# The mixer's steps in the paired heads: from between the parts of the scores to behind the softmax and behind the taking

## The chip, the cores and the metric

One core of one Trainium2 chip runs the whole program. The metric is the device time of one execution in microseconds (us); the time before is the median of three runs.

## The reference

A decode step for 8 batches: attention over a cache of 8192 keys and values for 32 query heads that share 8 key/value heads, beside an MLP-mixer over the one token, both added to the input. Everything is float32.

```python
B, Sq, D = 8, 1, 512;  Hq, Hkv, Sk, Dh = 32, 8, 8192, 128;  F = 1792

def _A_ref(x, k_cache, v_cache, wq, wo):
    q = (x @ wq).reshape(B, Sq, Hq, Dh).transpose(0, 2, 1, 3)
    k = jnp.repeat(k_cache, rep, axis=1)
    v = jnp.repeat(v_cache, rep, axis=1)
    scores = jnp.einsum("bhqd,bhkd->bhqk", q, k) * (Dh ** -0.5)
    p = _softmax(scores, axis=-1)
    o = jnp.einsum("bhqk,bhkd->bhqd", p, v)
    return o.transpose(0, 2, 1, 3).reshape(B, Sq, Hq * Dh) @ wo

def _B_ref(x, w1, b1, w2, b2):
    h = _layernorm(x, axis=-1)
    u = jnp.einsum("bsd,sf->bdf", h, w1) + b1
    u = _gelu(u)
    y = jnp.einsum("bdf,fs->bds", u, w2) + b2
    return y.transpose(0, 2, 1)

x = A_x
xn = _layernorm(x, axis=-1)
return x + _A_ref(xn, ...) + _B_ref(xn, ...)
```

The caches are 8 x 8 x 8192 x 128 numbers each, 4 MB for the keys of one batch and one head, and as much for the values.

## The kernel before

**Stages.** First the queries of all heads are made. Then come the paired heads: heads 0 to 5 are worked two at a time, which gives 24 steps `duo_step(i)`, i = 0 to 23, with pair `g = i // 8` and batch `b = i % 8`. Heads 6 and 7 follow one by one in `pair(i)`, and the last two batches are written out by hand at the end. The order of every engine's instructions is the order in which the code issues them.

**The ring.** Keys and values live in a ring of five slots of 4 MB (`raw`). One load of a paired step is the keys, or the values, of two heads: 8 MB, two slots. Where the two slots wrap around the end of the ring, the load is split into two of 4 MB. `load_next` puts the next load on SP's queue; it can start when the last reader of its slots is done. In a step it is called once between the two halves of the keys (this loads the next step's keys) and once behind the first half of the products with the values (the next step's values). In steps 2, 9, 10, 17 and 18 a smaller load of output weights (`load_wo`, 1 MB) goes out on the same queue.

**A paired step.** The keys come in two halves, k = 0 and 1, and each half in two quarters. For each quarter DVE turns two pieces in place (`turn_duo`, L480, two transposes of 128x2048), then PE multiplies them with the queries (`qk_duo`, L491, 8 matmuls). Behind the four quarters stands `softmax_duo`: DVE's maximum (L500), a matmul that spreads it (L502), DVE's bias (L504), the exponential on ACT (L508), two matmuls that rearrange the result (L511) and two transposes into `pt` (L512). Then PE multiplies with the values in two halves (`pv_duo`, L523), between which every fourth step places the results of the four steps before (`place_duo`), and some steps project them (`o_project`, whose addition to `yrow` on DVE is L469). `take_duo` copies the result on ACT (L531).

**The mixer.** For each batch and each of the 14 slices of F, `mx_step` runs a gelu on ACT (L574) and a multiplication and an addition on POOL (L575, L576) into `macc`. There are 8 x 14 = 112 such steps; `mix(n)` runs the next n of them wherever it is called. Where a batch is through, `mix` first issues `mx_end`: a matmul on PE that reads `macc` (L580) and an addition to `yrow` on DVE (L581). Then `mx_begin` spreads the next batch's row by a matmul (L566) into the one buffer `hb` that the gelus read, and clears `macc` on POOL (L568). The paired steps call four mixer steps each, 96 in all, so an `mx_end` falls in paired steps 3, 7, 10, 14, 17 and 21. The remaining 16 run in the single heads.

ACT holds one set of function tables at a time: a table load stands ahead of the first gelu behind an exponential and ahead of the exponential behind a gelu.

Of the kernel before, what the change touches and what calls it, by code (L numbers as in the profile page):

```python
# [44 lines left out]
def attn_mixer_kernel(ctx: ExitStack, tc: tile.TileContext, x, kc, vc, wq, wo, w1, b1, w2, b2, out):  # L45
# [22 lines left out]
    def misc():  # L68
        return ps_m.tile([P, 512], F32, name="misc")

    def big():
        return t2k.tile([P, 512], F32, name="t2k")
# [42 lines left out]
    def load_next():  # L115
        if duo:
            load_duo()
        elif order:
            _, src, to, i = order.pop()
            h, b = divmod(i, B)  # L120
            t = slot().rearrange("p s (t d) -> p (s t) d", d=DH)
            rows = src[b, h].rearrange("(p t) d -> p t d", p=P)
            last = not order
            at = 0
            for n in PIECES if last else (NT,):
                nc.sync.dma_start(t[:, at:at + n, :], rows[:, at:at + n, :])
                at += n
            to[i] = t
            if last:
                load_wo(HKV - 1)  # L130
# [3 lines left out]
    def load_wo(h):  # L134
        t = place.tile([P, REP, D], F32, name="wo")
        if h < PAIRED:
            rows = wo[h // 2 * 2 * REP * DH:(h // 2 + 1) * 2 * REP * DH, :].rearrange("(p c) n -> p c n", p=P)
            rows = rows[:, h % 2 * REP:(h % 2 + 1) * REP, :]
        else:
            how = "(r p) n -> p r n" if h == HKV - 1 else "(p r) n -> p r n"  # L140
            rows = wo[h * REP * DH:(h + 1) * REP * DH, :].rearrange(how, p=P)
        for r in range(REP) if h == HKV - 1 else ():
            nc.sync.dma_start(t[:, r, :], rows[:, r, :])
        if h < HKV - 1:
            nc.sync.dma_start(t, rows)
        wos[h] = t
# [177 lines left out]
    def q_place_duo(g):  # L324
        m = misc()
        for q in range(NB):
            for s in range(2):
                nc.tensor.matmul(m[s * HP:(s + 1) * HP, q * B * REP:(q + 1) * B * REP], rep[:, q, :HP],
                                 QT[:, 2 * g + s].rearrange("p b r -> p (b r)"), start=True, stop=True)
        z_fill(m, 0)  # L330
# [134 lines left out]
    def o_project(h):  # L465
        m = misc()
        for r in range(REP):
            nc.tensor.matmul(m[:W, :], OT[h][:, r, :], wos[h][:, r, :], start=(r == 0), stop=(r == REP - 1))  # L468
        nc.vector.tensor_add(yrow, m[:W, :], yrow)  # L469
# [8 lines left out]
    def turn_duo(i, c):  # L478
        k = KP[i][c // NCH][:, c % NCH * CH_T:(c % NCH + 1) * CH_T, :].rearrange("p t d -> p (t d)")
        nc.vector.transpose(k, k)  # L480
# [3 lines left out]
    def qk_duo(i, k, cs):  # L484
        b = i % B
        if not k and not cs[0]:
            SD[i] = ps_a.tile([P, 512], F32, name="acc")
        t = KP[i][k]
        for q in range(NB):
            for c in cs:  # L490
                nc.tensor.matmul(SD[i][c * W:(c + 1) * W, :].rearrange("p (t j) -> p t j", j=W),  # L491
                                 Z[:, q, b, (1 - k) * REP:(1 - k) * REP + W],
                                 t[:, c * CH_T:(c + 1) * CH_T, q * W:(q + 1) * W],
                                 start=(not k and not q), stop=(k == 1 and q == NB - 1))

    def softmax_duo(i):
        b = i % B
        s = SD.pop(i)
        mr = work.tile([P, 1], F32, name="mr")
        nc.vector.tensor_reduce(mr, s, AX.X, ALU.max)  # L500
        m = misc()
        nc.tensor.matmul(m[:, :P], mr.to_broadcast([P, P]), ident, start=True, stop=True)  # L502
        nb = work.tile([P, 1], F32, name="nb")
        nc.vector.tensor_tensor_reduce(big()[:, :P], m[:, :P], hmask, -SCALE, 3.0e38, ALU.add, ALU.min, nb)  # L504
        p = big()
        if b % HB == 0:
            LD[i // HB] = work.tile([P, HB], F32, name="lr4")
        nc.scalar.activation(p, s, AF.Exp, bias=nb, scale=SCALE, accum_out=LD[i // HB][:, b % HB:b % HB + 1])  # L508
        for k in range(2):
            m = misc()  # L510
            nc.tensor.matmul(m, send[:, k, :], p, start=True, stop=True)  # L511
            nc.vector.transpose(PT[k][:, :CH_T * W], m)  # L512
# [3 lines left out]
    def pv_duo(i, k):  # L516
        b = i % B
        if not k:
            OD[i] = ps_a.tile([P, 512], F32, name="acc")
        v = VP[i][k].rearrange("p (c t) d -> p t c d", c=NCH)  # L520
        for t in range(CH_T):
            j = t % NB
            nc.tensor.matmul(OD[i][j * W:(j + 1) * W, :].rearrange("p (c d) -> p c d", c=NCH),  # L523
                             PT[k][:, t * W:(t + 1) * W], v[:, t],
                             start=(not k and t < NB), stop=(k == 1 and t >= CH_T - NB))

    def take_duo(i):
        g, b = divmod(i, B)
        if b % HB == 0:
            OBD[g] = one.tile([P, HB, 512], F32, name="ob")  # L530
        nc.scalar.copy(OBD[g][:, b % HB, :], OD.pop(i))  # L531
# [21 lines left out]
    def place_duo(i):  # L553
        g, b = divmod(i, B)
        if b == 0:
            OT[2 * g], OT[2 * g + 1] = OTS
        if b % HB == HB - 1:
            s, rl = place_all(OBD.pop(g), LD.pop(i // HB), 2 * REP)
            for x in range(2):
                put(OTS[x], b - HB + 1, s[:, :, x * REP:(x + 1) * REP], rl)  # L560
# [3 lines left out]
    def mx_begin(b):  # L564
        hb = ps_h.tile([P, D], F32, name="hb")
        nc.tensor.matmul(hb, ident[:B, b:b + 1].to_broadcast([B, P]), hn, start=True, stop=True)  # L566
        acc = one.tile([P, D], F32, name="macc")
        nc.gpsimd.memset(acc, 0.0)  # L568
        mx[b] = (hb, acc)

    def mx_step(b, j):
        hb, acc = mx[b]
        g = one.tile([P, D], F32, name="g")
        nc.scalar.activation(g, hb, AF.Gelu_apprx_tanh, bias=b1t[:, j:j + 1], scale=w1t[:, j:j + 1])  # L574
        nc.gpsimd.tensor_scalar(g, g, w2t[:, j:j + 1], 1.0, op0=ALU.mult, op1=ALU.mult)  # L575
        nc.gpsimd.tensor_add(acc, acc, g)  # L576

    def mx_end(b):
        m = misc()
        nc.tensor.matmul(m[:W, :], bsel[:, BO - BS * b:BO - BS * b + W], mx[b][1], start=True, stop=True)  # L580
        nc.vector.tensor_add(yrow, m[:W, :], yrow)  # L581
# [4 lines left out]
    def mix(n):  # L586
        for _ in range(n):
            b, j = divmod(step[0], NF)
            step[0] += 1
            if j == 0 and 0 < b <= B:  # L590
                mx_end(b - 1)
            if b < B:
                if j == 0:
                    mx_begin(b)
                mx_step(b, j)
# [4 lines left out]
    def duo_step(i):  # L600
        g, b = divmod(i, B)
        half = NCH // 2
        for k in range(2):
            for x in range(2):
                for c in range(half):
                    turn_duo(i, k * NCH + x * half + c)
                qk_duo(i, k, range(x * half, (x + 1) * half))
                mix(1)
            if not k:
                load_next()  # L610
                if i == N_PR - 1:
                    load_next()
        if i == N_PR - 1:
            load_next()
        del KP[i]
        softmax_duo(i)
        if b == B - 1 and g < PAIRED // 2 - 1:
            q_place_duo(g + 1)
        pv_duo(i, 0)
        load_next()  # L620
        if i:
            place_duo(i - 1)
        if g and b == 1:
            o_project(2 * g - 2)
            load_wo(2 * g - 1)
        if g and b == 2:
            o_project(2 * g - 1)
        if b == 2:
            load_wo(2 * g)
        pv_duo(i, 1)  # L630
        if i == N_PR - 1:
            load_next()
        del VP[i]
        take_duo(i)

    for i in range(N_PR):
        duo_step(i)
# [139 lines left out]
```

## Time and profile before

| what | value |
|---|---|
| median of 3 runs | 1306.81 us (1306.71 to 1308.07) |
| the profiled execution's own time | 1306.54 us |
| its span, first to last instruction | 1304.6 us |
| mean granted TensorE clock | 0.863 |
| busy PE, DVE, ACT, POOL | 945.8, 701.1, 229.0, 229.6 us |
| read from HBM | 553.69 MB, 424 GB/s over the span |

The page's first part gives busy time by engine, its fourth the chain of waits that ended last: one goes back from the last instruction to what released it, and so on to the start. A row of the chain has a start, a length and what took it; "DMA raw<-in_A_k_cache_dram" is the time from the issue of a load to its landing. Windows give for a stretch of the span the busy time of each engine (and instructions), the clock that was granted to PE, the share of the 16 DMA engines and what they moved. In the timeline a row ends with the idle time ahead of the instruction and what ended it.

### The profile page before, as it was taken

The numbers are of one execution on the slowest core, as the hardware profiler recorded it, in microseconds if no ns is written. First come the engines' busy times: TensorE is split into PE (matmuls) and PEld (weight loads), VectorE is DVE, ScalarE is ACT, GpSimd is POOL, SyncE is SP. The second block draws the span as 40 slices with busy tenths as digits, with TensorE's granted clock in tenths as the row PEclk, the third lists the DMA queues.
The fourth block names the chain that finished last, engine by engine and source line by source line (L and its number), as shares of the span: only waits on it lengthen the run. The fifth ranks groups of instructions, "written<-read, shape, count | busy, mean of one in ns | idle before, by whom it ended". The sixth has DMA issues, their size and how long they took to land.

```text
span 1304.6 us, 11227 instructions
## 1 busy us (share of the span) xinstructions
PE 945.8 (72%) x4782; PEld 259.4 (20%) x4782; DVE 701.1 (54%) x581; ACT 229.0 (18%) x321; POOL 229.6 (18%) x247
## 2 busy tenths in 40 slices
PE   2767866867786886886778787687777674665778
PEld 0211211211221221221122121121122121211223
DVE  3554625652745553565445655346565654566575
ACT  0212121110222122021211221102121332310000
POOL 1222112220222112122211222102221312100000
PEclk9878888988898898887889898788887877878889
DMA  9999999999999999998999999998999999999998
GB/s 400 438 445 424 441 429 436 433 431 439 387 449 420 443 426 437 423 441 374 417 448 422 431 425 429 426 440 362 421 444 418 434 434 433 432 434 434 431 431 344
DMA packets 15925, 554.41 MB, mean 425 GB/s; under 512 B 1884, under 2 KB 1916, under 8 KB 2692
## 3 DMA queue, kind: packets, MB, share of 16 engines
q1 hardware_dynamic: 15732, 553.67, 98.7%
q8 instruction: 37, 0.61, 0.2%
q14 instruction: 12, 0.10, 0.0%
q0 software_dynamic: 128, 0.02, 0.0%
q10 hardware_dynamic: 16, 0.02, 0.0%
HBM read 553.69 MB, written 0.02 MB: 424 GB/s over the span
## 4 chain that ended last, share of the span: by engine, by line
DMA 53%; PE 24%; DVE 21%; ACT 1%; issue 1%; POOL 0%; DVEq 0%; ACTq 0%; POOLq 0%
DMA raw<-in_A_k_cache_dram 49%; DVE raw L480 16%; PE acc L491 12%; PE acc L523 3%; DVE raw L336 3%; PE acc L414 3%; PE misc L511 2%; DMA raw<-in_A_v_cache_dram 2%; DMA b2t<-in_B_b_dram 2%; PE misc L540 1%; PE acc L347 1%; DMA wo<-in_A_wo_dram 1%; PE misc L297 1%; ACT L508 1%; PE misc L468 1%
## 5 line engine op out<-in xcount | busy, mean ns | idle before, releaser
L491 PE MATMUL acc<-raw,z 128*32 128x512 f32 x1536 | 405.0, 663 | 161.3 <-DVE raw L480 158.0
L480 DVE STREAM_TRANSPOSE raw<-raw 128x2048 f32<-128x2048 f32 x192 | 424.5, 2272 | 144.1 <-DMA raw<-in_A_k_cache_dram 144.1
L575 POOL TENSOR_SCALAR g<-g,pad 128x512 f32<-128x512 f32 x112 | 77.4, 691 | 742.5 <-ACT g L574 742.5
L491 PEld LDWEIGHTS acc<-raw,z 128*32 128x32 f32 x1536 | 95.0, 119 | 469.0 <-issue 292.4
L523 PE MATMUL acc<-raw,pt 128*32 128x512 f32 x1536 | 188.0, 631 | 0.0
L336 DVE STREAM_TRANSPOSE raw<-raw 128x2048 f32<-128x2048 f32 x64 | 145.6, 2293 | 60.2 <-DMA raw<-in_A_k_cache_dram 60.2
L576 POOL TENSOR_TENSOR macc<-macc,g 128x512 f32<-128x512 f32 x112 | 142.3, 1270 | 9.3
L574 ACT ACTIVATE g<-hb,pad 128x512 f32<-128x512 f32 x112 | 87.0, 777 | 214.1 <-POOL macc L576 165.5
L511 PE MATMUL misc<-t2k,send 128*128 128x512 f32 x96 | 76.7, 944 | 56.5 <-ACT t2k L508 56.5
L512 DVE STREAM_TRANSPOSE pt<-misc 128x512 f32<-128x512 f32 x48 | 34.4, 717 | 106.7 <-PE misc L511 106.2
L347 PE MATMUL acc<-raw,z 128*32 128x512 f32 x512 | 80.6, 626 | 10.3 <-DVE raw L336 8.1
L523 PEld LDWEIGHTS acc<-raw,pt 128*32 128x32 f32 x1536 | 47.8, 116 | 144.8 <-issue 114.1
L414 PE MATMUL acc<-raw,pt 128*32 128x512 f32 x480 | 76.5, 776 | 0.0
L508 ACT ACT_TABLE_LOAD x24 | 30.8, 1283 | 220.0 <-DVE nb L504 219.9
L500 DVE TENSOR_REDUCE mr<-acc 128x1 f32<-128x512 f32 x24 | 16.6, 691 | 92.5 <-PE acc L491 92.5
L364 PE MATMUL misc<-ident,mr 128*128 128x128 f32 x32 | 10.6, 424 | 74.9 <-DVE mr L359 74.9
L531 ACT COPY ob<-acc 128x512 f32<-128x512 f32 x24 | 14.0, 585 | 285.5 <-PE acc L523 285.5
L574 ACT ACT_TABLE_LOAD x32 | 41.1, 1283 | 32.6 <-PE hb L566 32.1
L511 PEld LDWEIGHTS misc<-t2k,send 128*128 128x128 f32 x96 | 23.0, 263 | 79.9 <-ACT t2k L508 61.1
L381 ACT ACTIVATE t2k<-acc,nb 128x512 f32<-128x512 f32 x16 | 11.0, 687 | 135.8 <-DVE nb L370 135.7
L568 POOL MEMSET macc<- 128x512 f32 x8 | 4.2, 524 | 156.1 <-PE misc L580 137.3
L347 PEld LDWEIGHTS acc<-raw,z 128*32 128x32 f32 x512 | 18.9, 113 | 60.9 <-issue 41.7
(117 smaller groups left out, 362.7 us busy)
## 6 DMA issues: line engine op xcount, KB each, us to landing
raw<-in_A_k_cache_dram SPq DMA_DIRECT2D x26, 4096.0 KB, 27.9
raw<-in_A_v_cache_dram SPq DMA_DIRECT2D x25, 4096.0 KB, 27.1
raw<-in_A_k_cache_dram SPq DMA_DIRECT2D x4, 2048.0 KB, 33.1
wo<-in_A_wo_dram SPq DMA_DIRECT2D x7, 1024.0 KB, 26.2
raw<-in_A_v_cache_dram SPq DMA_DIRECT2D x3, 1024.0 KB, 22.1
raw<-in_A_v_cache_dram SPq DMA_DIRECT2D x2, 512.0 KB, 25.6
wo<-in_A_wo_dram SPq DMA_DIRECT2D x4, 256.0 KB, 16.3
raw<-in_A_v_cache_dram SPq DMA_DIRECT2D x19, 25.6
```

The lines of the kernel that those rows point to most:

```text
L336: nc.vector.transpose(k, k)
L347: nc.tensor.matmul(S[i][c * W:(c + 1) * W, :].rearrange("p (t j) -> p t j", j=W), Z[:, q, b, REP:], k[:, c * CH_T:(c + 1) * CH_T, q * W:(q ...
L414: nc.tensor.matmul(O[i][j * W:(j + 1) * W, :].rearrange("p (c d) -> p c d", c=NCH), pt[:, t * W:(t + 1) * W], v[:, t], start=(t < NB), sto ...
L480: nc.vector.transpose(k, k)
L491: nc.tensor.matmul(SD[i][c * W:(c + 1) * W, :].rearrange("p (t j) -> p t j", j=W), Z[:, q, b, (1 - k) * REP:(1 - k) * REP + W], t[:, c * C ...
L508: nc.scalar.activation(p, s, AF.Exp, bias=nb, scale=SCALE, accum_out=LD[i // HB][:, b % HB:b % HB + 1])
L511: nc.tensor.matmul(m, send[:, k, :], p, start=True, stop=True)
L512: nc.vector.transpose(PT[k][:, :CH_T * W], m)
L523: nc.tensor.matmul(OD[i][j * W:(j + 1) * W, :].rearrange("p (c d) -> p c d", c=NCH), PT[k][:, t * W:(t + 1) * W], v[:, t], start=(not k an ...
L574: nc.scalar.activation(g, hb, AF.Gelu_apprx_tanh, bias=b1t[:, j:j + 1], scale=w1t[:, j:j + 1])
L575: nc.gpsimd.tensor_scalar(g, g, w2t[:, j:j + 1], 1.0, op0=ALU.mult, op1=ALU.mult)
L576: nc.gpsimd.tensor_add(acc, acc, g)
```

## The change

In `duo_step` the call `mix(1)` behind each quarter of the scores is taken out. A call `mix(2)` is put behind `softmax_duo` and another behind `take_duo`. The mixer steps per paired step stay four, and each `mx_end` stays in its step.

```diff
                 for c in range(half):
                     turn_duo(i, k * NCH + x * half + c)
                 qk_duo(i, k, range(x * half, (x + 1) * half))
-                mix(1)
             if not k:
                 load_next()
...
         del KP[i]
         softmax_duo(i)
+        mix(2)
         if b == B - 1 and g < PAIRED // 2 - 1:
             q_place_duo(g + 1)
         pv_duo(i, 0)
...
         del VP[i]
         take_duo(i)
+        mix(2)
```

DVE in paired step 14 before (L480 turns the keys `raw`, L581 is the addition of `mx_end` to `yrow`, L500 and L504 begin the softmax):

```order
L480 STREAM_TRANSPOSE raw<-raw 128x2048 x2
L581 TENSOR_TENSOR yrow<-misc,yrow 32x512
L480 STREAM_TRANSPOSE raw<-raw 128x2048 x6
L500 TENSOR_REDUCE mr<-acc 128x1
L504 ISA t2k,nb<-misc,hmask 128x128
```

and DVE in the same step now (L512 turns the probabilities into the two tiles `pt`):

```order
L480 STREAM_TRANSPOSE raw<-raw 128x2048 x8
L500 TENSOR_REDUCE mr<-acc 128x1
L504 ISA t2k,nb<-misc,hmask 128x128
L504 ISA nb 128x1
L512 STREAM_TRANSPOSE pt_156<-misc 128x512
L512 STREAM_TRANSPOSE pt_158<-misc 128x512
L581 TENSOR_TENSOR yrow<-misc,yrow 32x512
```

The addition moved from behind the first two turnings to behind the last transpose of the softmax; steps 7 and 21 read alike.

PE in step 14 before (L491 the scores, L580 the matmul of `mx_end`, L566 that of `mx_begin`, L502 and L511 those of the softmax):

```order
L491 MATMUL acc<-raw,z 32x512 x8
L580 MATMUL misc<-macc,bsel 32x512
L566 MATMUL hb<-hn,ident 128x512
L491 MATMUL acc<-raw,z 32x512 x24
L502 MATMUL misc<-ident,mr 128x128
```

and PE in the same step now (L523 the products with the values):

```order
L491 MATMUL acc<-raw,z 32x512 x32
L502 MATMUL misc<-ident,mr 128x128
L511 MATMUL misc<-t2k,send 128x512 x2
L580 MATMUL misc<-macc,bsel 32x512
L566 MATMUL hb<-hn,ident 128x512
L523 MATMUL acc<-raw,pt_156 32x512 x16
```

The two matmuls moved from between the scores to between the softmax and the products with the values.

DVE from the softmax of step 17 to the first turnings of step 18 now (L469 is the addition of `o_project`):

```order
L504 ISA nb 128x1
L512 STREAM_TRANSPOSE pt_156<-misc 128x512
L512 STREAM_TRANSPOSE pt_158<-misc 128x512
L469 TENSOR_TENSOR yrow<-misc,yrow 32x512
L581 TENSOR_TENSOR yrow<-misc,yrow 32x512
L480 STREAM_TRANSPOSE raw<-raw 128x2048 x8
```

where before step 17 had L581 within its own turnings, six of them ahead of it and two behind:

```order
L480 STREAM_TRANSPOSE raw<-raw 128x2048 x6
L581 TENSOR_TENSOR yrow<-misc,yrow 32x512
L480 STREAM_TRANSPOSE raw<-raw 128x2048 x2
L500 TENSOR_REDUCE mr<-acc 128x1
L504 ISA t2k,nb<-misc,hmask 128x128
```

The addition moved to behind the taking of step 17, ahead of the turnings of step 18; step 10 reads alike, and step 3 without an L469. The orders of POOL and SP did not change.

## The prediction

> **What bounds the kernel now.** I read the page first, then the chain of waits, then windows of 10 us, then the timeline around the places where the windows dip.
>
> ```profile
> q1 hardware_dynamic: 15732, 553.67, 98.7%
> DMA 53%; PE 24%; DVE 21%; ACT 1%; issue 1%; POOL 0%; DVEq 0%; ACTq 0%; POOLq 0%
> ```
>
> The loads on SP's queue fill 98.7% of the span, so only places where that queue runs empty can be won. In an undisturbed step the chain looks so (start, length, what):
>
> ```profile
> 278.22 4.52 DVE raw L480 x2
> 282.78 8.02 PE acc L491 x32
> 290.81 25.96 DMA raw<-in_A_k_cache_dram
> 316.87 4.51 DVE raw L480 x2
> ```
>
> The keys of paired step 6 are there at 278.22, those of step 7 at 316.87: 38.65 us for one load of keys and one of values, 19.3 each. The load of keys 7 is issued at 290.81, 12.6 after keys 6 came, when PE has read their first half (k=0). Steps 14 and 21 (the last three rows) look otherwise:
>
> ```profile
> 596.10 4.52 DVE raw L480 x2
> ...
> 605.39 0.68 DVE yrow L581
> ...
> 610.54 6.54 PE acc L491 x17
> 617.10 22.95 DMA raw<-in_A_k_cache_dram
> 640.13 4.52 DVE raw L480 x2
> ...
> 800.02 4.52 DVE raw L480 x2
> ...
> 840.99 17.67 DVE raw L480 x8
> ...
> 900.54 23.19 DMA raw<-in_A_k_cache_dram
> 923.83 4.52 DVE raw L480 x2
> ```
>
> Here `mx_end`'s addition to yrow (L581) stands between the turnings of keys: DVE waits from about 600.6 to 605.39 until PE is through the first quarter's scores and the product of `mx_end`, and the next load is issued 21.0 us after the keys came instead of 12.6. It then finds the queue empty: 22.95 and 23.19 us from issue to landing, where a load that follows another takes 19.3. So **a load costs nothing if it is issued 23.1 before it is due**: keys at 38.65 - 23.1 = 15.5 after the keys before (2.9 spare in step 6), values at 58.0 - 23.1 = 34.9 after the keys of the step that issues them. The windows (busy by engine, granted clock, DMA share, GB/s) show the holes:
>
> ```profile
> 340.00:350.00 10.00, 6.56 (x19) 2.16 (x16) 1.59 (x4) 2.06 (x3) 0.00 (x0) 0.84 1.01 433
> 350.00:360.00 10.00, 10.00 (x93) 3.25 (x94) 9.39 (x6) 2.65 (x6) 0.00 (x0) 0.99 0.96 383
> 610.00:620.00 10.00, 9.42 (x36) 2.58 (x38) 9.25 (x5) 2.33 (x3) 6.54 (x7) 0.68 0.57 216
> 750.00:760.00 10.00, 10.00 (x69) 2.80 (x62) 3.71 (x4) 0.11 (x1) 0.00 (x0) 1.00 0.98 390
> 890.00:900.00 10.00, 6.91 (x23) 1.71 (x25) 10.00 (x5) 3.61 (x4) 5.72 (x6) 0.66 0.59 256
> ```
>
> All four holes lie in or right behind a step with an `mx_end` (steps 7, 14, 17, 21). Steps 3 and 10 have one too, and spare time to swallow it.
>
> **The change, part by part.** The 96 mixer steps stay, four to a paired step, two behind the softmax and two behind the taking. Six `mx_end`s with the `mx_begin` behind them move: in steps 7, 14, 21 to behind the softmax, in 3, 10, 17 to behind the taking. In step 14 (the rows of DVE and PE stand with the change) all eight turnings of the keys now run without a wait for PE. L580 and L566 left the scores (L491) and stand ahead of the products with the values (L523), and the next load of values waits for those. Their price, and the marks I need, from the timeline:
>
> ```profile
> 299.59 0.69 DVE L500 TENSOR_REDUCE mr<-acc 128x1 f32<-128x512 f32 x1 [3.71 <-PE acc L491]
> 343.41 0.69 DVE L500 TENSOR_REDUCE mr<-acc 128x1 f32<-128x512 f32 x1 [3.71 <-PE acc L491]
> 354.91 0.33 SPq L105 DMA_DIRECT2D raw<-in_A_v_cache_dram  x1
> 717.52 13.28 DVE L480 STREAM_TRANSPOSE raw<-raw 128x2048 f32<-128x2048 f32 x6 [0.17 <-DMA raw<-in_A_k_cache_dram]
> 744.84 0.69 DVE L500 TENSOR_REDUCE mr<-acc 128x1 f32<-128x512 f32 x1 [5.19 <-PE acc L491]
> 753.02 0.33 SPq L105 DMA_DIRECT2D raw<-in_A_v_cache_dram  x1
> 880.73 4.50 DVE L480 STREAM_TRANSPOSE raw<-raw 128x2048 f32<-128x2048 f32 x2
> 887.89 0.59 PE L580 MATMUL misc<-macc,bsel 128*32 128x512 f32 x1
> 888.84 1.12 PE L566 MATMUL hb<-hn,ident 8*128 8x512 f32 x2
> 906.56 0.69 DVE L500 TENSOR_REDUCE mr<-acc 128x1 f32<-128x512 f32 x1 [3.71 <-PE acc L491]
> 916.37 0.33 SPq L105 DMA_DIRECT2D raw<-in_A_v_cache_dram  x1
> ```
>
> L580 and L566 take PE from 887.89 to 889.96, with one pass of scores among them (0.25, as 32 passes take 8.02 in step 6): 1.8 us, bounded above by twice that, 3.6, at half clock, and below by nothing, if PE only fills a wait with them. The softmax begins (L500) 299.59 - 278.22 = 21.4 after the keys in a step without a stall. Now step by step:
>
> - Step 7. Before, values 8 were issued at 354.91, landing 378.0, due 316.87 + 58.0 = 374.9: 3.1 lost. Now L500 comes at 338.3, 5.1 earlier, and the issue at 354.91 - 5.1 + 1.8 = 351.6 (353.4 at the upper price), landing at 374.7 (376.5): 0 lost (up to 1.6). Gain 3.1, at least 1.5.
> - Step 14. 640.13 - 596.10 - 38.65 = 5.4 lost. Now the keys are issued at 596.10 + 12.6 = 608.7, land by 631.8, due 634.8: gain 5.4.
> - Step 17. Values 18: 753.02 + 23.1 = 776.1, due 717.5 + 58.0 = 775.5, 0.6 lost. L500 comes 744.84 - 738.9 = 5.9 earlier: gain 0.6. By the keys it may be more: 800.02 - 717.52 = 82.5 for two steps, less 77.3, less 2.4 for the 1 MB of `wo` among them (an eighth of a load), is 2.8.
> - Step 21. 923.83 - 840.99 - 77.3 = 5.5 lost. Now keys 22 go out at 880.73 + 12.6 = 893.3, land by 916.4, due 840.99 + 77.3 = 918.3. Values 22 followed L500 by 9.8; now 902.1 + 9.8 + 1.8 = 913.7 (915.5), landing 936.8 (938.6), due 937.6: 0 lost (up to 1.0). Gain 5.5, at least 4.5.
> - Steps 3, 10: nothing was lost, nothing is gained.
>
> The sum is 3.1 + 5.4 + 0.6 + 5.5 = 14.6, at least 12.0, at most 16.8 with step 17's 2.8. Counted in undone bytes against 433 GB/s the four windows give (50 + 217 + 43 + 177) / 433 x 10 = 11.2. The first counts a late landing whole, part of which the queue may make good later; the second misses what lies outside the windows. I take 13.5, nearer to the landings, since the chain goes over these.
>
> What moves at no cost: the gelus on ACT between exponential and taking.
>
> ```profile
> 272.53 0.58 ACT L531 COPY ob<-acc 128x512 f32<-128x512 f32 x1 [9.13 <-PE acc L523]
> 273.13 1.28 ACT L574 ACT_TABLE_LOAD   x1
> ...
> 277.37 0.78 ACT L574 ACTIVATE g<-hb,pad 128x512 f32<-128x512 f32 x1 [2.17 <-POOL macc L576]
> ```
>
> A table load, two gelus and the wait for POOL are 5.0 us, inside the 9.13 that ACT idles before it takes; were they longer, the taking would be late, which frees one of four accumulators and holds no load. The tables still change twice a step. POOL's and SP's orders are unchanged. At step 7 the copies of the next heads' queries follow the gelus, ready before the products with the values end.
>
> Behind the taking (3, 10, 17) the addition waits for all products with the values, and the next keys' turnings are queued behind it on DVE. In step 17 L469, `o_project`'s addition, waited there already; L581 is what joined it.
>
> ```profile
> 200.93 4.50 DVE L480 STREAM_TRANSPOSE raw<-raw 128x2048 f32<-128x2048 f32 x2 [14.84 <-DMA raw<-in_A_k_cache_dram]
> 756.41 0.68 DVE L469 TENSOR_TENSOR yrow<-misc,yrow 32x512 f32<-32x512 f32 x1 [6.29 <-PE misc L468]
> 757.02 17.64 DVE L480 STREAM_TRANSPOSE raw<-raw 128x2048 f32<-128x2048 f32 x8
> 759.64 1.02 PE L491 MATMUL acc<-raw,z 128*32 128x512 f32 x2
> ```
>
> Behind step 17 PE ends about 759.6 - 5.9 = 753.7; with 1.8 and 0.7 the turnings begin near 756, not later than the 757.02 of before. Behind step 3 DVE idles 14.84 for the keys anyway. No cost.
>
> **The rivals.**
>
> *The clock eats half of it.* In step 14 the second quarter-scores took 6.54 in a window of clock 0.68, against 8.02 for two quarters in step 6: after a stall PE ran at half rate. If L580, L566 and the first products with the values all meet the half rate, the issue of values 8 and 22 is later by 1.8 + 2.5 (6.54 less half of 8.02): landing 379.0 and 941.1, 4.1 and 3.5 late, the sum 14.6 - 7.6 = 7.0, the time 1299.5. For it: PE idles through the exponential. Against it: the added products themselves fill PE there. The Trainium skill, "TensorE: Matmul & The Clock Gate", Part 1, says that an idle window of about 3.4 us halves the rate and a busy one restores it; the 0.68 beside 6.54 agrees. By that rule this rival needs an idle window ahead of L580; without one the sum stays. 12%.
>
> *The addition behind the taking holds the keys* (slower). If at 3, 10 and 17 DVE stood from the end of L512 to the end of PE's products, 6.3 (the wait of L469) + 3.2 (from its end of wait to 759.64) + 1.8 = 11.3, while the keys lay ready, each next load of keys would be 11.3 late, 2.9 of it spare: 8.4 x 3 = 25, less 14.6, so 1306.5 + 10.5 = 1317. It decides from keys that land over 4 us before PE is done. For it: L469's 6.29 shows this kind of hold. Against it: 14.84 in step 4, and the estimate of 756. The skill's same page (Part 1, "Architectural detail") has VectorE strictly first in, first out; the wait at 605.39 agrees. 6%.
>
> *Nothing comes of it.* The queue was 98.7% busy; what is not lost in the holes might be lost at other loads whose spare time the holes had refilled. Then 1306, within 2.6 us. Against it: the chain starts from a landing in each step, so all behind a hole shifts as one. 5%.
>
> **How the numbers follow.** The profiled execution took 1306.54, span 1304.6 and 1.9 outside, 0.3 under the median of 1306.81. 1306.5 - 13.5 = 1293.0, the likeliest case, 77%. Its own range is 1306.5 - 16.8 = 1290 to 1306.5 - 11.2 = 1295; with the clock's rival it reaches 1300, which leaves 11% out. Within 0.2%, 2.6 us, no change can be told. Faster 0.89, same 0.05, slower 0.06.
>
> **What would show it.** Right: no window of 10 us in the paired part under 400 GB/s; keys loads in steps 14 and 21 issued 12 to 13 after the keys; the wait of L581 for PE gone from the chain. The clock's rival: values 8 or 22 issued over 36 after their keys. The slower one: L480 behind L581 with no idle for keys, and new holes at steps 4, 11, 18. Wrong altogether: holes gone and the span unchanged.

## The result, and the profile after

The changed kernel takes 1294.13 us, the median of 4 runs (1293.01 to 1296.09), beside 1307.44 of the kernel before (4 runs, 1306.71 to 1308.79): a ratio of 0.9899, 95% interval 0.9882 to 0.9916. In a later comparison on one chip (experiment 10 below) it was 0.9905 (0.9885 to 0.9925). The forecast was 1293.0 in 1290 to 1300.

The profiled execution of after took 1296.09 us with a span of 1293.6, the longest of its four. From its page, the queue's row:

```profile
q1 hardware_dynamic: 15732, 553.67, 99.3%
```

The same 15,732 packets and 553.67 MB; the loads' share rose from 98.7% to 99.3%. The busy times of the engines changed little (PE 945.8 to 934.9 us, DVE 701.1 to 701.6): the kernel was bound by its loads and still is, with fewer holes. The chain around steps 14 and 21 (start, length, what):

```profile
595.68 4.51 DVE raw L480 x2
600.24 8.02 PE acc L491 x32
608.28 25.96 DMA raw<-in_A_k_cache_dram
634.33 4.52 DVE raw L480 x2
...
834.15 17.68 DVE raw L480 x8
...
873.62 4.41 DVE raw L480 x2
...
886.11 25.38 DMA raw<-in_A_k_cache_dram
911.58 4.52 DVE raw L480 x2
```

These now read like the undisturbed step 6: 32 passes of scores in one piece of 8.02, no L581 between, the next keys asked for 608.28 - 595.68 = 12.6 us after the keys came, and 634.33 - 595.68 = 38.65 us from keys to keys. Before, the distance was 44.03 there. At step 21, 911.58 - 834.15 = 77.4 for two steps, where 82.8 stood. The windows that had shown the holes, and one that still dips (busy by engine, granted clock, DMA share, GB/s):

```profile
350.00:360.00 10.00, 10.00 (x86) 3.01 (x78) 9.59 (x5) 3.73 (x8) 6.13 (x7) 1.00 1.07 455
430.00:440.00 10.00, 4.84 (x22) 0.80 (x16) 5.27 (x3) 2.05 (x3) 3.92 (x4) 0.74 0.90 390
610.00:620.00 10.00, 6.74 (x30) 1.64 (x26) 4.33 (x5) 1.29 (x2) 0.00 (x0) 1.00 1.00 433
890.00:900.00 10.00, 7.14 (x25) 1.94 (x22) 3.43 (x6) 0.78 (x2) 0.00 (x0) 1.00 1.00 433
```

The 216 and 256 GB/s of 610 to 620 and 890 to 900 are 433 now, the 383 at 350 is 455. The same work runs up to 12 us earlier in after, so a window does not hold quite the same piece of it; but between 270 and 960 us after has no window under 390. The timeline of after at two of the new places, step 7 (behind the softmax) and step 17 (behind the taking):

```profile
345.48 1.29 PE L580 MATMUL misc<-macc,bsel 128*32 128x512 f32 x2
346.70 1.12 PE L566 MATMUL hb<-hn,ident 8*128 8x512 f32 x2
346.81 0.68 DVE L581 TENSOR_TENSOR yrow<-misc,yrow 32x512 f32<-32x512 f32 x1 [0.50 <-PE misc L580]
352.04 0.33 SPq L105 DMA_DIRECT2D raw<-in_A_v_cache_dram  x1
...
749.99 0.68 DVE L581 TENSOR_TENSOR yrow<-misc,yrow 32x512 f32<-32x512 f32 x1 [3.61 <-PE misc L580]
750.60 17.64 DVE L480 STREAM_TRANSPOSE raw<-raw 128x2048 f32<-128x2048 f32 x8
```

Behind the softmax L581 waits 0.50 us for PE in step 7, where the first half of the next keys is already there (their turnings begin at 347.42, at once behind it). In steps 14 and 21 it waits 0.26, and the next keys come some 10 us later. Behind the taking of step 17 it still waits 3.61, and the turnings of the next keys, which lie ready, start at once behind it. In total VectorE (DVE in the rows) does not wait much less for this product. Groups of waits (total us, count, longest), before and then after:

```profile
DVE yrow L581 <- PE misc L580: 31.6, 8, 5.8
```

```profile
DVE yrow L581 <- PE misc L580: 23.8, 8, 8.1
```

7.8 us of waiting went, and 13 us of time: the gain must lie in which loads stand behind a wait more than in how long the engine waits. (In experiment 1 the sum is 6.9, and the time that of after.)

**Where the time came from.** One step's distance from keys to keys scatters by more than 1 us between executions, so I take stretches of the arrival of keys (the first turning, L480) that hold the moved work of one or two steps: keys 7, 11, 15, 19, 22. Those of before are 316.87, 477.53, 640.13, 800.02 and 923.83; of the profiled execution of after 316.90, 477.35, 634.33, 793.16 and 911.58. Keys 9 and 11 in the timeline of before and in the chain of after:

```profile
397.45 4.50 DVE L480 STREAM_TRANSPOSE raw<-raw 128x2048 f32<-128x2048 f32 x2 [7.64 <-DMA raw<-in_A_k_cache_dram]
...
477.53 17.64 DVE L480 STREAM_TRANSPOSE raw<-raw 128x2048 f32<-128x2048 f32 x8
```

```profile
395.91 4.52 DVE raw L480 x2
...
447.33 30.00 DMA raw<-in_A_k_cache_dram
477.35 4.52 DVE raw L480 x2
```

The chain of a second profiled execution of after (experiment 10, 1293.36 us, the lowest of its five runs, but nearer to the median):

```profile
316.75 17.68 DVE raw L480 x8
...
395.50 8.90 DVE raw L480 x4
...
446.80 28.37 DMA raw<-in_A_k_cache_dram
475.19 4.52 DVE raw L480 x2
...
593.60 8.90 DVE raw L480 x4
633.63 4.52 DVE raw L480 x2
...
791.01 4.52 DVE raw L480 x2
...
910.62 4.52 DVE raw L480 x2
```

| stretch | moved work in it | before | after | after again | gain (two executions) | forecast |
|---|---|---|---|---|---|---|
| keys 7 to 11 | steps 7, 10 | 160.66 | 160.45 | 158.44 | 0.2, 2.2 | 3.1 |
| keys 11 to 15 | step 14 | 162.60 | 156.98 | 158.44 | 5.6, 4.2 | 5.4 |
| keys 15 to 19 | step 17 | 159.89 | 158.83 | 157.38 | 1.1, 2.5 | 0.6 |
| keys 19 to 22 | step 21 | 123.81 | 118.42 | 119.61 | 5.4, 4.2 | 5.5 |
| sum | | 606.96 | 594.68 | 593.87 | 12.3, 13.1 | 14.6 |

The first row needs a second look. From keys 7 to keys 9, which hold step 7 alone, the three executions took 80.58, 79.01 and 78.75: 1.6 and 1.8 won, nearly the same twice. What sets the two executions of after apart comes later: the load of keys 11 went out 12.6 us after keys 10 (434.73 and 434.21) in both, and took 30.00 us in the one and 28.37 in the other. In before, keys 11 may have come a little before 477.53, since that row shows no wait for a load: the engine was at an addition of `o_project` until then.

### The profile page after: what moved, and what is told of

It reads as the page before. It is cut to its first block, busy times and chain, and to the rows that moved or that the text cites. A ratio compares the mean times of both kernels' runs of the same rounds, so it can differ in the third digit from the quotient of the medians.

```text
span 1293.6 us, 11227 instructions
## 1 busy us (share of the span) xinstructions
PE 934.9 (72%) x4782; PEld 258.5 (20%) x4782; DVE 701.6 (54%) x581; ACT 225.6 (17%) x320; POOL 230.1 (18%) x247
## 3 DMA queue, kind: packets, MB, share of 16 engines
q1 hardware_dynamic: 15732, 553.67, 99.3%
## 4 chain that ended last, share of the span: by engine, by line
DMA 52%; PE 24%; DVE 20%; ACT 1%; issue 1%; POOL 0%; DVEq 0%; ACTq 0%; POOLq 0%
DMA raw<-in_A_k_cache_dram 48%; DVE raw L480 15%; PE acc L491 11%; PE acc L523 3%; PE acc L414 3%; DVE raw L336 3%; PE misc L511 2%; DMA b2t<-in_B_b_dram 2%; DMA raw<-in_A_v_cache_dram 2%; PE acc L347 1%; PE misc L540 1%; DMA wo<-in_A_wo_dram 1%; PE misc L297 1%; PE misc L468 1%; ACT L508 1%
## 5 line engine op out<-in xcount | busy, mean ns | idle before, releaser
L491 PE MATMUL acc<-raw,z 128*32 128x512 f32 x1536 | 395.5, 647 | 159.4 <-DVE raw L480 154.3
L480 DVE STREAM_TRANSPOSE raw<-raw 128x2048 f32<-128x2048 f32 x192 | 424.1, 2274 | 145.3 <-DMA raw<-in_A_k_cache_dram 145.2
L491 PEld LDWEIGHTS acc<-raw,z 128*32 128x32 f32 x1536 | 93.2, 116 | 460.1 <-issue 287.3
L523 PE MATMUL acc<-raw,pt 128*32 128x512 f32 x1536 | 181.6, 613 | 0.0
L576 POOL TENSOR_TENSOR macc<-macc,g 128x512 f32<-128x512 f32 x112 | 142.4, 1271 | 9.3
L511 PE MATMUL misc<-t2k,send 128*128 128x512 f32 x96 | 75.3, 931 | 56.5 <-ACT t2k L508 56.5
L574 ACT ACTIVATE g<-hb,pad 128x512 f32<-128x512 f32 x112 | 87.2, 779 | 139.6 <-POOL macc L576 119.9
L512 DVE STREAM_TRANSPOSE pt<-misc 128x512 f32<-128x512 f32 x48 | 34.4, 717 | 105.3 <-PE misc L511 104.4
L347 PE MATMUL acc<-raw,z 128*32 128x512 f32 x512 | 83.7, 652 | 10.0 <-DVE raw L336 7.8
L414 PE MATMUL acc<-raw,pt 128*32 128x512 f32 x480 | 75.3, 765 | 0.0
L523 PEld LDWEIGHTS acc<-raw,pt 128*32 128x32 f32 x1536 | 47.6, 113 | 135.4 <-issue 107.5
L500 DVE TENSOR_REDUCE mr<-acc 128x1 f32<-128x512 f32 x24 | 16.6, 692 | 89.1 <-PE acc L491 89.1
L574 ACT ACT_TABLE_LOAD x31 | 39.8, 1283 | 14.6 <-PE hb L566 14.1
L511 PEld LDWEIGHTS misc<-t2k,send 128*128 128x128 f32 x96 | 23.0, 262 | 80.8 <-ACT t2k L508 61.1
L381 ACT ACTIVATE t2k<-acc,nb 128x512 f32<-128x512 f32 x16 | 11.0, 687 | 134.7 <-DVE nb L370 134.6
L508 ACT ACTIVATE t2k<-acc,nb 128x512 f32<-128x512 f32 x24 | 16.5, 687 | 89.7 <-DVE nb L504 89.5
```

Source lines behind the costliest of these rows:

```text
L347: nc.tensor.matmul(S[i][c * W:(c + 1) * W, :].rearrange("p (t j) -> p t j", j=W), Z[:, q, b, REP:], k[:, c * CH_T:(c + 1) * CH_T, q * W:(q ...
L414: nc.tensor.matmul(O[i][j * W:(j + 1) * W, :].rearrange("p (c d) -> p c d", c=NCH), pt[:, t * W:(t + 1) * W], v[:, t], start=(t < NB), sto ...
```

## The experiments

Theory, as predicted: a load is lost only where it is issued too late for its turn in the queue; what counts is VectorE's wait ahead of turnings on which a load hangs. "The rule" below is the prediction's: a load costs nothing up to 15.5 us (keys) or 34.9 us (values) after the keys of the step that issues it. Rivals: the products ahead of the values cost PE time; the gelus' place (ScalarE and GpSimd, ACT and POOL in the rows) matters; the addition behind the taking holds the keys. All kernels are compared with the kernel before on the same chip, which had medians of 1306.52 (experiments 1 to 4), 1307.68 (5 to 8) and 1307.58 (9 to 12). Where a median is set against that of after, it is the 1293.96 of experiment 10; for 1 to 8 that was another chip, and a difference of such medians is good to 1 to 2 us.

**1. Before, with the addition alone moved** (in the paired steps). All else stays among the scores: L580, L566 and the gelus.

```
 def mx_end(b):
-    nc.vector.tensor_add(yrow, m[:W, :], yrow)
+    late.append(m)          # add_late() issues it behind the step's last turning
 ...
     turn_duo(i, k * NCH + x * half + c)
+if k and x: add_late()
 qk_duo(...)
 mix(1)
```

> The kernel before, with one thing moved: the addition of mx_end to yrow on DVE (L581 of before) is issued behind the last turning of the step instead of between the turnings; its matmul, mx_begin and all gelus stay between the scores. Theory (the loss was DVE's wait for PE between the turnings, which sent the next load of keys out late): the keys' loads of steps 14 and 21 go out 12.6 to 14.4 us after their keys, the holes close, 1294 to 1296 us, ratio to before 0.990 to 0.992. Rival one (moving the gelus and their work on POOL away from the turnings brought the gain): 1305 to 1308, ratio 0.998 to 1.001. Rival two (half of the loss is the clock of PE and the two matmuls among the scores): about 1300, ratio 0.995.

Measured: 1293.68 us (1293.21 to 1295.23, 4 runs), ratio 0.9898 (0.9872 to 0.9924). Its chain at step 14, and its row of waits for the product (L582 and L586 are L581 and L580 of before):

```profile
593.97 4.51 DVE raw L480 x2
598.52 4.89 PE acc L491 x13
603.85 1.05 PE hb L566 x2
...
608.50 25.29 DMA raw<-in_A_k_cache_dram
633.88 8.90 DVE raw L480 x4
```

```profile
DVE yrow L582 <- PE misc L586: 6.9, 2, 5.3
```

The matmuls of the mixer still stand between the scores and cost the keys' load 2 us (issued 14.5 after the keys, not 12.6), within its spare time; keys 15 come 39.9 after keys 14, as in the second execution of after (40.0). The time is that of after. So the wait of one addition on VectorE is the whole effect, as far as the runs can tell; whether matmuls, gelus and table loads stand among the scores or in their new places changes nothing that can be measured. (A third place for the gelus does cost time: experiment 5.)

**2. After, with the three ends of 7, 14 and 21 back behind the first quarter of the scores.**

```
+def turn_over():            # mx_end and mx_begin alone, where one is due
+    ...
 qk_duo(i, k, ...)
+if not k and not x and i: turn_over()
```

> The changed kernel, with mx_end and mx_begin of steps 7, 14 and 21 put back behind the first quarter of the scores; all gelus stay behind the softmax and the taking. Theory: the holes of steps 7, 14 and 21 come back, 1.6 to 3.1 + 5.4 + 5.5 us more than the changed kernel, 1306 to 1308, ratio to before 0.998 to 1.001. Rival one (the gelus' place): as the changed kernel, 1293 to 1295, ratio 0.99. Rival two (clock): as the theory.

Measured: 1304.06 us (1300.8 to 1305.11, 10 runs), ratio 0.9967 (0.995 to 0.9984). Its chain at step 14 is that of before again:

```profile
596.09 4.51 DVE raw L480 x2
600.65 4.52 PE acc L491 x13
605.68 0.68 DVE yrow L581
...
615.85 23.00 DMA raw<-in_A_k_cache_dram
```

The load goes out 19.8 after the keys, 4.3 past the 15.5 of the rule, and the next keys come 42.85 after, 4.2 more than 38.65. The holes are back (275 GB/s at 610 to 620, 315 at 890 to 900). So these three hold most of the gain: 1304.06 - 1293.96 (after in experiment 10) = 10.1 us by the medians, (0.9967 - 0.9899) x 1307 = 8.9 by the ratios. Expected were 12.5 to 14.0, so 2.4 to 5.1 are missing. That left steps 3, 10 and 17 to look at (experiment 9).

**3. Only step 14 back** (the same edit with `i == 14`).

> The changed kernel, with mx_end and mx_begin put back behind the first quarter of the scores in step 14 alone. Theory: one hole, 5.4 us more than the changed kernel, 1299 to 1300, ratio to before 0.994; in the trace the next keys land 44 instead of 38.7 us after those of step 14, and later steps keep the distance. Rival one: ratio 0.99. If the queue could make a late landing good later, less than 3 us more.

Measured: 1297.68 us (1297.46 to 1297.85, 5 runs), ratio 0.9928 (0.9904 to 0.9952). Its chain at step 14:

```profile
594.07 4.51 DVE raw L480 x2
...
614.85 23.09 DMA raw<-in_A_k_cache_dram
638.04 2.31 DVE raw L480
```

The load goes out 20.8 after the keys (5.3 past the rule's 15.5), and the next keys come 43.97 after, 5.3 more than 38.65. Here the rule is exact, yet the time is 3.7 above that of after (3.0 to 3.8 by the ratios): a late landing is not worth its whole length at the end. In the profiles, after loses more elsewhere in these stretches (in its second execution keys 14 to 15 took 633.63 - 593.60 = 40.0, although the load was issued 12.6 after keys 14).

**4 and 11. The first two mixer steps behind the first products with the values** and the load behind these, so that L580 and L566 no longer stand ahead of it.

```
 softmax_duo(i)
-mix(2)
 ...
 pv_duo(i, 0)
 load_next()
+mix(2)
```

> The changed kernel, with the first mix(2) moved on, from behind the softmax to behind the first half of the products with the values and the load that follows it. Theory: in step 7 the load of values 8 goes out about 2.3 us earlier (the 1.22 and 1.05 us of L580 and L566 are no longer ahead of it), so up to 1.7 us of what step 7 still loses comes back: 1292.5 to 1294, ratio to before 0.9885 to 0.9895. If the price of the two matmuls on the load of values was nothing: as the changed kernel, ratio 0.990.

> The kernel with the first mix(2) behind the first half of the products with the values, beside the changed kernel on one chip. Theory: 0 to 1.7 us faster than the changed kernel, most likely 0.5, ratio to before 0.0005 lower. If all that is left is the rate of the loads: no difference.

Measured: 1293.52 us (1293.24 to 1293.67, 4 runs), ratio 0.9894 (0.9869 to 0.992), and in the second comparison 1293.81 us (5 runs), 0.9905 (0.9882 to 0.9928), beside 1293.96 of after on the same chip. Values 8 go out 33.0 and 33.1 after keys 7, against 35.1 and 33.5 in two profiled executions of after, and it makes no difference in the time: the price of L580 and L566 is covered.

**5. All four steps behind the taking.**

```
 softmax_duo(i)
-mix(2)
 ...
 take_duo(i)
-mix(2)
+mix(4)
```

> The changed kernel, with mix(2) behind the softmax taken out and mix(4) behind the taking. Theory (what counts is when the loads of keys and values go out): the ends of steps 7, 14 and 21 are harmless there. Those of steps 3, 10 and 17 now stand behind two gelus: PE waits for POOL about 7 us after the taking, DVE's addition with it, and the next keys' turnings behind that. Step 4's keys come later anyway; in steps 11 and 18 the keys lie ready, their next loads of keys go out 6 to 7 us later, 3 and 2 us past their spare time: 1297 to 1300 us, ratio to before 0.992 to 0.995. If the addition behind the taking held no keys: ratio 0.990.

Measured: 1299.47 us (1297.38 to 1301.34, 4 runs), ratio 0.9936 (0.9911 to 0.9961): about 5.5 more than after. In the timeline at the end of step 17:

```profile
759.92 1.91 PE L580 MATMUL misc<-macc,bsel 128*32 128x512 f32 x2 [7.89 <-POOL macc L576]
761.87 0.68 DVE L581 TENSOR_TENSOR yrow<-misc,yrow 32x512 f32<-32x512 f32 x1 [12.56 <-PE misc L580]
775.05 0.33 SPq L105 DMA_DIRECT2D raw<-in_A_k_cache_dram  x1
```

Two gelus now run just ahead of the product. It waits 7.89 for GpSimd's sum, the addition 12.56 for the product, and the next load of keys goes out at 775.05, where after has 763.17. That is the slower rival's mechanism, and it is real. In after the gelus that the product needs lie behind the softmax, so GpSimd is done before the products with the values are.

**6. After without the gelus.** `mx_step` (L574 to L576) is left out in the paired steps.

> The changed kernel without the mixer's gelus, multiplications and additions (ACT and POOL) in the paired steps; mx_end and mx_begin stay, so the mixer's part of the output is not computed there. Theory: where they stand now they are hidden behind the products with the values and behind the wait for keys: 1292.5 to 1294.5, ratio to before 0.989 to 0.9905. Rival (they still slow DVE, PE or the loads by what they read and write): over 3 us faster than the changed kernel, ratio under 0.988.

Measured: 1293.8 us (1293.66 to 1294.3, 4 runs), ratio 0.9893 (0.9873 to 0.9914). ScalarE's busy time falls from 226 to 94 us and GpSimd's from 230 to 41, and the time stays. Where they stand in after they cost nothing, as forecast.

**7, 8 and 12. How much room is left.** In each step a piece of the keys is turned twice more ahead of the scores, which delays both loads of the step.

```
+def turn_again(i):
+    k = KP[i][0][:, :CH_T, :].rearrange("p t d -> p (t d)")[:, :1024]   # 8: 2048, 12: 512
+    for _ in range(2):
+        nc.vector.transpose(k, k)
 ...
+if not k and not x: turn_again(i)
 qk_duo(...)
```

> The changed kernel, with half of the first piece of keys turned twice more in each paired step, ahead of the first quarter of the scores (the data end as they were): about 2.3 us more on DVE in each of 24 steps, 55 us in all. Theory (a load is free if it goes out 23.1 us before it is due): keys go out 14.9 after the keys before, within 15.5, values near 34.9 at their limit of 34.9: 0 to 0.5 us a step, 1294 to 1304 us, ratio to before 0.990 to 0.998. If there is no such spare time: 1294 + 24 x 2.3 = 1348, ratio 1.03.

> The changed kernel, with the whole first piece of keys turned twice more in each paired step, ahead of the first quarter of the scores: about 4.5 us more on DVE in each of 24 steps, 109 us in all. Theory: keys go out 17.1 after the keys before, 1.6 past the limit of 15.5, so a step takes 40.1 to 40.3 instead of 38.65 us where the load is not split by the ring's end: 1320 to 1332, ratio to before 1.010 to 1.020. If the spare time were larger than the 23.1 says: ratio 0.99; if there were none: 1294 + 109, ratio 1.07.

> The changed kernel, with a quarter of the first piece of keys turned twice more in each paired step: about 1.2 us more on DVE in each, 29 us in all. If a load is free up to 15.5 us behind the keys (it goes out at 13.8 here): as the changed kernel, 1294, ratio 0.990. If the edge is soft, as 1311 at 2.3 us suggests: 1296 to 1302, ratio 0.991 to 0.996.

Measured: 1311.2 us (1309.01 to 1315.79, 10 runs), ratio 1.0025 (1.0011 to 1.004) with about 2.3 us more per step; 1341.42 us (1336.54 to 1348.2, 4 runs), 1.0256 (1.0208 to 1.0305) with about 4.5; 1299.54 us (1294.72 to 1306.01, 11 runs), 0.9945 (0.9925 to 0.9965) with about 1.2. One step from the chain of 7 (L485 is the first of the two added turnings), and one from that of 8:

```profile
403.23 4.50 DVE raw L480 x2
407.73 1.14 DVE raw L485
...
418.23 23.54 DMA raw<-in_A_k_cache_dram
441.86 4.50 DVE raw L480 x2
```

```profile
290.86 4.50 DVE raw L480 x2
...
307.99 23.64 DMA raw<-in_A_k_cache_dram
331.73 4.50 DVE raw L480 x2
```

In 8 the load goes out 17.1 after the keys and lands 23.64 later, 40.87 from keys to keys: 2.2 over 38.65. If some 22 steps lose as much, that is 49; measured are 47. The rule with its 23.1 would have given 1.6. In 7 the load goes out at 15.0, inside the rule's 15.5, and this step keeps its 38.63; but the values' loads, also later, now go out 34.8 to 36.2 after the keys in half of the steps, at or past the rule's 34.9, and the time is 17 above after. That it is these loads which cost the 17 us is argued from their times and not shown by a run. I had both too low, by 7 at the nearest in 7 and by 9 in 8. The room is thus under about 2 us per step, and 12 shows that the edge is not sharp: 1.2 us more cost 5.6 in the median and scattered 11 runs over 11 us, where the 4 and 5 of after lie within 3.1 and 1.0 (and 15 of before over 7.8).

The lateness need not be all of it. The granted clock of PE was lower too: 0.852, 0.855 and 0.850 in the profiled executions of 12, 7 and 8, 0.872 in that of experiment 10. In 12 the scores of the first half took 8.4 to 8.8 us in several steps, where 8.02 stands in after; in step 6 the load of keys so went out 14.4 after the keys and not at the 13.8 that I had worked out. No run separates the two.

**9. After, with the ends of 3, 10 and 17 back behind the third quarter**, each with its two gelus ahead of it.

```
+if i in (3, 10, 17):
+    if not k: mix(1)
+    elif not x: turn_over()
 ...
 take_duo(i)
-mix(2)
+if i not in (3, 10, 17): mix(2)
```

> The changed kernel, with the ends of steps 3, 10 and 17 alone put back: their mx_end and mx_begin stand behind the third quarter of the scores as before, with the two gelus that they need ahead of them. Theory: only step 17 had too little spare time, so 0.6 to 2.8 us more than the changed kernel, 1295 to 1297 us, ratio to before 0.990 to 0.992; with the three others (measured: 1304.06) the two parts add up to the whole change. If these three ends cost nothing: ratio as of the changed kernel in this call.

> The changed kernel once more, as the mark for the others of this call: 1293 to 1295 us, ratio to before 0.990.

Measured: 1297.0 us (1296.35 to 1298.44, 5 runs), ratio 0.993 (0.9909 to 0.995), against 1293.96 (1293.36 to 1294.37, 5 runs), 0.9905 (0.9885 to 0.9925) of after (run 10): 3.0 us. Its timeline in step 17:

```profile
728.49 0.68 DVE L581 TENSOR_TENSOR yrow<-misc,yrow 32x512 f32<-32x512 f32 x1 [3.75 <-PE misc L580]
749.84 0.33 SPq L105 DMA_DIRECT2D raw<-in_A_v_cache_dram  x1
```

The addition waits 3.75, the softmax begins late (L500 at 740.01), and values 18 go out 38.4 after keys 17 (which came at 711.46), 3.5 past the rule's 34.9. Keys 17 to 19 take 83.6, in after 80.4. In before the same load went out 35.5 after and keys 17 to 19 took 82.5, so this kernel overdraws step 17 by about 1 us; 2 of its 3 are what before lost there.

Experiments 2 and 9 together give 10.1 + 3.0 = 13.1 by the medians, 8.9 + 3.0 = 11.9 with the ratios, of 13.6 us (1307.58 - 1293.96); about 1 us of either is that overdraft, so 1.5 to 2.7 us of the whole are not placed.

## Why the prediction was right, point by point

- **What bounds it, and the rule for late loads:** right. The load's issue moved to 12.6 after the keys at 14 and 21. Where a load was put back past 15.5 (experiments 2 and 3), the next keys came later by what the rule says: 4.3 by the rule and 4.2 measured, 5.3 and 5.3. Near the edge it is too kind, by 0.2 to 0.7 us a step if the cost is spread over 24 steps (experiments 12, 7 and 8): the loads of keys shown there took 23.54 and 23.64 from issue to landing, not 23.1.
- **Step 14 (5.4) and step 21 (5.5):** the mechanism right, the size somewhat high: 5.6 and 5.4 in the first profile, 4.2 and 4.2 in the second, 3.7 in time for step 14 alone (experiment 3). The landing view counts each late landing whole.
- **Step 7 (3.1, at least 1.5):** the mechanism right, the size too high, at the lower bound: 1.6 and 1.8 by keys 9. Values 8 were forecast at 351.6 and went out at 352.04, 35.1 after the keys, and in the second profile at 350.24, 33.5 after. (There L511's product of the softmax, ahead of L580, took 1.98, in the first 3.39, as it did before.) "0 lost" behind that was wrong: keys 9 are due 77.3 after keys 7 and came 79.01 and 78.75 after, so about 1.5 us are still lost. Even in experiments 4 and 11, with values 8 out at 33.0 and 33.1, they came 78.1 and 78.6 after. Why is open. The 0.2 of the table's first row is not step 7's: 1.4 us of it went between keys 9 and 11.
- **Step 17 (0.6, by the keys 2.8):** this term was mis-sized. It gave 1.1 and 2.5, and up to 3.0 by experiment 9. I had taken the landing of values 18 against its due time, 0.6 late, and left the keys' 2.8 only in the upper bound; the keys were nearer: from keys 17 to 19 after took 80.4 and 79.9, 2.1 and 2.6 less than before.
- **The sum:** 14.6 with a choice of 13.5, measured 13.3 to 13.6. That the choice came within 0.2 is luck in part: it lies between two views (11.2 and 14.6) of which neither was shown to be the right one, and the excess at 7, 14 and 21 was partly made up by the shortfall at 17.
- **No cost of the gelus, of L580 and L566 ahead of the values, of the turnings behind step 17:** right, by experiments 6, 4 and 11. The turnings began at 750.60, forecast near 756; it was earlier since the whole step had moved up.
- **The rivals:** the clock did not take half. L580 and L566 took 1.29 + 1.12 at step 7, and moving them away changed nothing. The addition behind the taking does wait (3.61 at 749.99), and experiment 5 shows what it costs when GpSimd is still behind it; in after this is covered. Experiment 1, where no L581 stands there, turned keys 18 at 746.52 and sent the load of keys 19 out at 759.09, both 4 us earlier than after, and still needed 79.7 from keys 17 to 19, where after needs 80.4 and 79.9. "Nothing comes of it" fell with the windows and the time.
- **Signs that were wrong:** The wait of L581 for PE is not gone from the chain: at step 17 it still goes over L580 and L581 to the turnings at 750.60. These follow L581 with no idle for keys, which was named as a sign of the slower rival; no new hole came behind it, and it cost 0.7 us at the most. And "no window of 10 us under 400 GB/s": three stay at 390 to 396, among them 430 to 440 with a share of 0.90. Before had 383 there too: a dip of a tenth is not by itself the mark of a late load; the two that were, at steps 14 and 21, had shares of 0.57 and 0.59.

## What to carry to other kernels

Where the queue of loads is the bound, ask of each in-order engine what a load has to wait for: the price of a wait is decided by the loads that stand behind it more than by its length, and moving one addition of 0.68 us behind the last turning of the step was worth as much as moving the whole block. Work out from the trace how early a load must be issued to cost nothing, and leave 2 to 3 us beyond it: the keys' loads have 2.9 here, and with 1.2 us more work in each step time was lost. Size a change by stretches of several steps and by a second profile, since one step's distance scatters by as much as a term of the sum.

## What was not expected of the hardware

Loads issued just in time were not free here: 1.2 us of work more per step, by the rule still almost free, cost 5.6 us and spread 11 runs from 1294.72 to 1306.01; how much of that is the queue and how much the lower clock of PE is open. The same four matmuls of the softmax (L511, step 7), after the same idle time of 2.65, took 3.39 us in one execution of after and 1.98 in another, with a granted clock of 0.83 and 1.00 in the window of 340 to 350. What decides between the two was not settled.
